# Strassen's method for the third layer, packed values as 64x32 matmuls, and a filler removed, in a one-core attention and MoE kernel

## The chip, the core and the metric

The kernel runs on one core of one Trainium2 chip. The core has TensorE (PE in the profile) for matmuls, VectorE (DVE), ScalarE (ACT) and GpSimd (POOL) for element work, and queues that issue DMA transfers between HBM and the on-chip SBUF; in this kernel the loads and stores are issued from SyncE (SP). Matmuls write to PSUM, which has eight banks of 128 partitions by 512 fp32 values here. The metric is the device time of one execution in microseconds (us), lower is better; it is given as the median of several runs.

## The reference

```python
def sm_attn(qq, kk, vv):                         # scale = 1/sqrt(64)
    s = scale * qq @ kk.transpose(0, 1, 3, 2)
    a = np.exp(s - max(s)); a = a / (sum(a) + 1e-9)
    return a @ vv
p_packed = sm_attn(p, k, v)                      # 8 x 8 heads, 32 packed rows, 576 tokens, depth 64
out = sm_attn(q, p_packed, p_packed)             # 8 x 8 heads, 576 tokens
x = out.transpose(0, 2, 1, 3).reshape(4608, 512)
h = x @ w_in                                     # layer 1: 512 -> 2048
x = (h * np.cos(h)) @ w_out                      # layer 2: 2048 -> 512
h = x @ w2_in                                    # layer 3: 512 -> 2048
return (h * tanh(softplus(h))) @ w2_out          # mish, then layer 4: 2048 -> 512
```

All data are fp32. The kernel makes a product of two fp32 matrices from three matmuls in a rounded fp32 form: each operand is split into a high part (a cast) and a low part (the subtraction of that cast), and high x high, high x low and low x high are added in PSUM. The helper `mm3` (lines 139 to 142) issues these three, so nearly all matmuls of the profile stand on lines 140, 141 and 142.

## The kernel before, in words

**Stage A** covers attention and layers 1 and 2. It runs 256 steps: 16 token blocks t of 288 tokens times 16 tiles s of 128 hidden features. A step issues `l1` (6 matmuls of 288 columns) and, three steps later (`LAG_A`), `l2` (12 matmuls of 288 columns). Between the two stands a chain for each step: an ACT pass (L709), two DVE passes (L711, L712), the sine on ACT (L718), a DVE product (L719), an ACT cast (L726) and a POOL subtraction (L729), whose result `gh` layer 2 needs. The attention output is never multiplied out before layer 1: the packed values of a batch entry (32 x 64 for each head) are multiplied with layer 1's weights first, in `w_unit` (L492, plain fp32), and ACT and DVE split the result (L503, L504) into the `wab` tiles that layer 1 reads. Loads, element passes and matmuls of attention, of these units and of the weight preparation are put into tables by step (`at_ld`, `at_ew`, `at_pe`); a scheduler that uses priorities then orders the instructions of each engine.

Weights of layers 3 and 4 are loaded, rounded and written to DRAM tiles (`ws`) in stage A (`pre2`), and late in stage A `w2_load` reads them back and splits them. Layer 3's 16 pieces then stay in eight `wab` tiles, layer 4's 16 in `wo` tiles. **Stage B** covers layers 3 and 4: 9 blocks of 512 tokens times 16 tiles of hidden features. A step has `l3` (12 matmuls of 512 columns), mish on ACT, a split, and three steps later `l4` (12 matmuls of 512 columns). So stage B has 9 x 16 x 24 = 3456 matmuls of 512 columns, half of them for layer 3. While it runs, the next token block's `x` is loaded from DRAM, split, and the results of a finished block are copied out of PSUM and stored.

Of the kernel before, what the change touches and what calls it, by code (L numbers as in the profile page):

```python
# [56 lines left out]
W_D = 0  # L57
X2_AT = 250
# [17 lines left out]
PERM = ((0, 1, 2, 3), (2, 3, 0, 1))  # L76


def build(tc, q, k, v, p, w1i, w1o, w2i, w2o, out):
    nc = tc.nc  # L80
    ctx = ExitStack()
    with ctx:
# [29 lines left out]
        mask = wpool.tile([128, 64], F32, name="mask")  # L112
        nc.vector.memset(mask, 0.0)
        for a in range(2):
            nc.vector.memset(mask[64 * a : 64 * a + 64, 32 * a : 32 * a + 32], 1.0)
# [40 lines left out]
        PS = {}  # L156
        PW = {}
        lastexp = [None]

        def k_unit(b, g, alloc_v):  # L160
# [135 lines left out]
            def s6_ew():  # L296
                if b not in PS:
                    PS[b] = ap.tile([128, 128], F32, tag="psp", bufs=3, name=nm("psp"))
                nc.scalar.copy(PS[b][64 * g : 64 * g + 64], st["xt"][64 * g : 64 * g + 64, :128])
                if (b // 2, g) not in PW:  # L300
                    PW[(b // 2, g)] = ap.tile([128, 2, 2, D], F32, tag=f"pw{g}", bufs=2 - g, name=nm("pw"))
                pw = PW[(b // 2, g)]
                for sp in range(2):
                    i = sp if par == 0 else 1 - sp
                    nc.vector.tensor_tensor(pw[:, i, sp], st["xt"][:, 64 * sp : 64 * sp + 64], mask, ALU.mult)
# [14 lines left out]
        def q_unit(t, pre=None):  # L320
# [28 lines left out]
            def s2_pe():  # L349
                st["s"] = [ring() for _ in range(2)]  # L350
                for l in range(4):
                    h = PERM[b % 2][l]
                    for g in range(2):
                        nc.tensor.matmul(  # L354
                            st["s"][g][32 * l : 32 * l + 32, :TT],
                            PS[b][64 * g : 64 * g + 64, 32 * l : 32 * l + 32],
                            st["kt"][64 * g : 64 * g + 64, TT * h : TT * h + TT],
                            start=True,
                            stop=True,
                        )  # L360
# [103 lines left out]
        whalf = {}  # L464

        def w_unit(pair, fg, hp, bp, fresh=False, m=None):
            st = {} if m is None else m
            g, i = hp // 2, hp % 2
            cs = []

            if fresh:
# [8 lines left out]
                cs = cs[:-1]  # L480
            else:

                def load():
                    st["m"] = ld_tile([128, 512])
                    nc.sync.dma_start(st["m"], w1s[(fg, hp)])

            def pe():
                if i == 0:
                    whalf[(bp, fg, g)] = ring()
                ps = whalf[(bp, fg, g)]  # L490
                pos = bp ^ i
                nc.tensor.matmul(  # L492
                    ps[64 * pos : 64 * pos + 64], PW[(pair, g)][:, i, pos], st["m"], start=True, stop=True
                )

            def ew():
                if i == 0:
                    return
                ps = whalf.pop((bp, fg, g))
                w = W1.get((2 * pair + bp, fg))  # L500
                if w is None:
                    w = W1[(2 * pair + bp, fg)] = wab_tile(bp, [128, 2, 2, 512], F32R)
                nc.scalar.copy(w[:, g, 0], ps)  # L503
                nc.vector.tensor_tensor(w[:, g, 1], ps, w[:, g, 0], ALU.subtract)  # L504

            return load, cs, pe, ew
# [16 lines left out]
        W2 = {}  # L523

        def w2_load(key):
            st = {}

            def load():
                st["r"] = ld_tile([128, 512])
                nc.sync.dma_start(st["r"], w2s[key])  # L530

            def hi():
                if key[0] == "i":
                    _, j, c = key
                    if j not in W2:
                        W2[j] = wab_tile(j // 4, [128, 2, 2, 2, 256], F32R)
                    v = W2[j][:, c].rearrange("p l a f -> p l (a f)")
                else:
                    v = WO[(2, key[1])] = wo_tile([128, 2, 512], F32R)
                st["v"] = v  # L540
                nc.scalar.copy(v[:, 0], st["r"])

            def lo():
                eng = nc.gpsimd if key[-1] % 3 == 0 else nc.vector
# [61 lines left out]
        place(stages, [PRO + Q0_T + i for i in range(2)] + [PRO + Q0 + i for i in range(6)], HP_PRO)  # L606
        for j in range(16):
            load, cs, pe, ew = w_unit(0, j // 4, j % 4, 0, True)
# [4 lines left out]
            at_pe(n, pe)  # L613
            at_ew(n, ew)
# [12 lines left out]
        for j in range(16):  # L627
            load, cs, pe, ew = w_unit(0, j // 4, j % 4, 1)
            n = W01[0] + int(W01[1] * j)
            at_ld(n - W_LD, load)  # L630
            at_pe(n, pe)
            at_ew(n, ew)
# [18 lines left out]
        for pair in range(3):  # L651
# [9 lines left out]
            for j in range(16):  # L661
                m = {}
                n = n0 + W_POS[pair][0] + int(W_POS[pair][1] * (j // 2 * 2 + 1))
                at_ld(n - W_LD - 1 + j % 2, w_unit(pair + 1, j // 4, j % 4, 0, m=m)[0])
                for bp in range(2):
                    _, _, pe, ew = w_unit(pair + 1, j // 4, j % 4, bp, m=m)
                    at_pe(n + W_D * bp, pe)
                    at_ew(n + W_D * bp, ew)
# [5 lines left out]
        n0 = 192  # L674
        for j in range(8):
            for c in range(2):
                n = n0 + 33 + 2 * j + c if j < 4 else n0 + 48 + 4 * (j - 4) + 2 + c
                load, hi, lo = w2_load(("i", j, c))
                at_ld(n, load)
                at_ew(n + 1, hi)  # L680
                at_ew(n + 2, lo)
# [233 lines left out]
```

## Time and profile before

| | before |
|---|---|
| median of 3 runs | 1654.02 us (1653.84 to 1654.74) |
| the profiled execution's own time | 1651.3 us |
| its span, first to last instruction | 1649.5 us |
| PE busy | 1588.2 us, 96% of the span |
| DVE, ACT, POOL busy | 717.9, 762.2 and 365.0 us |
| mean granted TensorE clock | 0.992 of full speed |

The span leaves out 1.8 us of the execution's own time. The median lies 2.7 us above the time of the profiled execution. A busy share says only how long an engine had work in flight; which engine sets the end is read from the chain that ended last and from the gaps of that engine.

### The profile page before, as it was taken

What the parts mean: (1) busy time and instruction counts of PE and PEld (TensorE: products, weight loads), DVE (VectorE), ACT (ScalarE), POOL (GpSimd) and SP (SyncE); (2) the same over time, 40 slices, a digit from 0 to 9 for tenths busy, and PEclk for the clock granted to TensorE, in tenths of its full rate; (3) what the DMA queues carried; (4) which work ended last, traced back from release to release, by engine and by line L of the source; (5) the groups of instructions that cost most, each with busy time, mean ns of one, the idle gap of its engine ahead of it and who ended that gap; (6) DMA issues with size and microseconds to landing.
All of it is one profiled execution on the core that took longest, in us unless ns stands there. A gap on an engine that the chain in (4) does not pass through costs nothing.

```text
span 1649.5 us, 25389 instructions
## 1 busy us (share of the span) xinstructions
PE 1588.2 (96%) x9568; PEld 1324.5 (80%) x9568; DVE 717.9 (44%) x1529; ACT 762.2 (46%) x1510; POOL 365.0 (22%) x376
## 2 busy tenths in 40 slices
PE   3879999999999999999999999999999999999999
PEld 1667777799878997889898888888888888888887
DVE  5986665666657666687761111111111111111111
ACT  3676576666656666667772222322222222222221
POOL 0552223343323333244660010101010101000000
PEclk9899999999999999999999999999999999999999
DMA  9979565533544343353340010101010101010000
GB/s 285 305 192 237 152 189 135 136 79 86 162 113 99 89 124 127 98 187 117 111 131 0 16 36 1 52 0 51 1 52 1 51 0 52 1 52 1 8 18 26
DMA packets 101115, 147.42 MB, mean 89 GB/s; under 512 B 25728, under 2 KB 51328, under 8 KB 100992
## 3 DMA queue, kind: packets, MB, share of 16 engines
q1 hardware_dynamic: 100992, 145.79, 31.1%
q8 instruction: 75, 1.23, 0.3%
q14 instruction: 48, 0.39, 0.1%
HBM read 114.29 MB, written 31.46 MB: 88 GB/s over the span
## 4 chain that ended last, share of the span: by engine, by line
PE 84%; DMA 7%; DVE 4%; ACT 2%; issue 2%; SPq 1%; POOL 0%; DVEq 0%; ACTq 0%; POOLq 0%
PE acc L140 15%; PE acc L141 14%; PE acc L142 14%; PE ps L140 12%; PE ps L141 11%; PE ps L142 11%; PE ps L492 3%; DMA kr<-in_k_dram 1%; DMA kr<-in_q_dram 1%; DMA raw<-in_moe_w_out_dram 1%; PE ps L354 1%; DMA ld<-ws 1%; PE ps L214 1%; PE ps L275 1%; DVE r L719 1%
## 5 line engine op out<-in xcount | busy, mean ns | idle before, releaser
L856 DVE TENSOR_TENSOR gh<-gg,gh 128x512 fp32r<-128x512 f32 x144 | 105.7, 734 | 623.6 <-ACT gh L855 623.5
L849 ACT ACTIVATE gg<-ps 128x512 f32<-128x512 f32 x144 | 86.1, 598 | 550.4 <-PE ps L142 550.4
L729 POOL TENSOR_TENSOR gh<-r,gh 128x288 fp32r<-128x288 f32 x256 | 215.6, 848 | 396.4 <-ACT gh L726 288.6
L141 PE MATMUL acc<-gh,wo 128*128 128x288 f32 x1024 | 301.9, 300 | 0.3
L142 PE MATMUL acc<-gh,wo 128*128 128x288 f32 x1024 | 297.8, 298 | 0.0
L140 PE MATMUL acc<-gh,wo 128*128 128x288 f32 x1024 | 284.3, 305 | 1.7 <-ACT gh L726 1.7
L141 PE MATMUL acc<-wo,gh 128*128 128x512 f32 x576 | 227.2, 394 | 0.0
L140 PE MATMUL acc<-wo,gh 128*128 128x512 f32 x576 | 226.7, 394 | 0.0
L142 PE MATMUL acc<-wo,gh 128*128 128x512 f32 x576 | 225.0, 391 | 0.0
L140 PEld LDWEIGHTS acc<-gh,wo 128*128 128x128 f32 x1024 | 184.7, 190 | 38.7 <-issue 18.0
L141 PEld LDWEIGHTS acc<-gh,wo 128*128 128x128 f32 x1024 | 194.6, 190 | 8.8 <-issue 4.6
L142 PEld LDWEIGHTS acc<-gh,wo 128*128 128x128 f32 x1024 | 193.4, 190 | 6.3 <-issue 4.6
L140 PE MATMUL ps<-aT,wab 128*128 128x288 f32 x512 | 160.5, 314 | 17.0 <-DVE r L719 10.9
L718 ACT ACTIVATE r<-r,halfpi 128x288 f32<-128x288 f32 x256 | 135.7, 535 | 78.4 <-DVE r L712 75.9
L709 ACT ACTIVATE ki<-ps,quarter 128x288 int32<-128x288 f32 x256 | 125.5, 496 | 83.4 <-PE ps L142 73.4
L141 PE MATMUL ps<-aT,wab 128*128 128x288 f32 x512 | 152.9, 299 | 0.0
L142 PE MATMUL ps<-aT,wab 128*128 128x288 f32 x512 | 152.5, 298 | 0.0
L719 DVE TENSOR_TENSOR r<-r,ps 128x288 f32<-128x288 f32 x256 | 113.9, 449 | 69.1 <-ACT r L718 68.7
L711 DVE SCALAR_TENSOR_TENSOR r<-ki,ps 128x288 f32<-128x288 int32 x256 | 113.9, 448 | 55.8 <-ACT ki L709 46.5
L140 PEld LDWEIGHTS ps<-aT,wab 128*128 128x128 f32 x512 | 97.9, 192 | 39.1 <-DVE r L719 20.2
L140 PEld LDWEIGHTS acc<-wo,gh 128*128 128x128 f32 x576 | 108.2, 188 | 25.1
L142 PEld LDWEIGHTS acc<-wo,gh 128*128 128x128 f32 x576 | 108.2, 188 | 24.8
(124 smaller groups left out, 2579.2 us busy)
## 6 DMA issues: line engine op xcount, KB each, us to landing
ld<-ws SPq DMA_DIRECT2D x96, 256.0 KB, 2.9
kr<-in_k_dram SPq DMA_DIRECT2D x64, 272.0 KB, 5.7
raw<-in_moe_w_out_dram SPq DMA_DIRECT2D x32, 512.0 KB, 4.8
kr<-in_q_dram SPq DMA_DIRECT2D x60, 272.0 KB, 5.5
x2d<-xo SPq DMA_DIRECT2D x64, 144.0 KB, 1.8
out_dram<-ld SPq DMA_DIRECT2D x36, 256.0 KB, 2.0
raw<-in_moe_w_in_dram SPq DMA_DIRECT2D x16, 512.0 KB, 5.7
ws<-tmp SPq DMA_DIRECT2D x32, 256.0 KB, 4.8
```

The lines of the kernel that those rows point to most:

```text
L140: nc.tensor.matmul(ps, l0, r0, start=first, stop=False)
L141: nc.tensor.matmul(ps, l0, r1, start=False, stop=False)
L142: nc.tensor.matmul(ps, l1, r0, start=False, stop=last)
L214: nc.tensor.matmul(st["s1"][x][32 * l : 32 * l + 32, :TT].rearrange("p (s a) -> p a s", a=9), st["pp"][64 * x : 64 * x + 64, 32 * h : 32 * ...
L492: nc.tensor.matmul(ps[64 * pos : 64 * pos + 64], PW[(pair, g)][:, i, pos], st["m"], start=True, stop=True)
L709: nc.scalar.activation(ki, st["h"], AF.Identity, bias=quarter, scale=1.0 / TWO_PI)
L711: nc.vector.scalar_tensor_tensor(r, ki, -TWO_PI, st["h"], ALU.mult, ALU.add)
L718: nc.scalar.activation(g, g, AF.Sin, bias=halfpi, scale=1.0)
L719: nc.vector.tensor_tensor(g, g, st["h"], ALU.mult)
L729: nc.gpsimd.tensor_tensor(gh[:, 1], st["g"], gh[:, 0], ALU.subtract)
L849: nc.scalar.activation(g, st["h"], AF.Mish)
L856: nc.vector.tensor_tensor(gh[:, 1], st["g"], gh[:, 0], ALU.subtract)
```

## The change

It has three parts.

**Layer 3 by Strassen's method** (in Winograd's form). The product of a 512 x 256 piece of the weights with 1024 tokens is cut into 2 x 2 blocks on each side. Instead of eight block products, seven are made from sums of blocks, and the four result blocks are sums of the seven. There are now four token blocks of 1024 and one of 512. For each, and for each of 8 pairs p of hidden tiles, `product` issues 7 x 6 matmuls (of 512 columns, in the last block of 256) where 48 stood for the same 1024 tokens. DVE adds the products out of PSUM. The hidden values of a block's second 512 tokens are kept in 16 `G` tiles, and layer 4 for them runs behind all pairs (`xs`, `g_split`, the loop over `f`). The weight sums are made in stage A by `w2_comb`, eight units, seven steps apart from step 180: two loads, four DVE sums, four splits into `raw` tiles and four writes to DRAM tiles `wst`. Stage B streams them: `ws_load` fetches 256 KB for each product into one of five `tmp` buffers, 280 times, and the load for product m+5 is issued behind product m. The sums of x are made by `x_units`, at the end of stage A for the first block, later in the second part of the block ahead.

**Packed values as 64x32 matmuls.** `PK` is one ACT copy of 128 x 128 per batch entry and group, without the mask and its DVE products. A unit now issues four matmuls with 64 rows and 32 columns of the array for one batch entry, or eight for two, where matmuls with 128 rows and 64 columns, half of them masked to zero, stood.

**A filler removed.** `gap_b`, 48 unused values per partition, is gone.

```diff
-X2_AT = 250
+X2_AT = 248
+COMB = (180, 7)
-PERM = ((0, 1, 2, 3), (2, 3, 0, 1))
+PERM = ((0, 2, 1, 3), (1, 3, 0, 2))
...
-                    pw = PW[(b // 2, g)]
-                    nc.vector.tensor_tensor(pw[:, i, sp], st["xt"][:, 64 * sp : 64 * sp + 64], mask, ALU.mult)
+                PK[(b, g)] = ap.tile([128, 128], F32, tag=f"pk{g}", bufs=4, name=nm("pk"))
+                nc.scalar.copy(PK[(b, g)], st["xt"][:, :128])
...
-                nc.tensor.matmul(
-                    ps[64 * pos : 64 * pos + 64], PW[(pair, g)][:, i, pos], st["m"], start=True, stop=True
-                )
+                for x in range(4):
+                    for b in bs:
+                        for l, h in enumerate(PERM[b % 2]):
+                            if l == x:
+                                r = 64 * (h % 2)
+                                nc.tensor.matmul(
+                                    st[b][32 * l : 32 * l + 32],
+                                    PK[(b, g)][r : r + 64, 32 * l : 32 * l + 32],
+                                    ms[h // 2]["m"][r : r + 64],
...
+        def w2_comb(j):
...
+            def sums():
+                c0, c1 = st["c"]
+                a11, a21, a12, a22 = c0[:, :, :128], c0[:, :, 128:], c1[:, :, :128], c1[:, :, 128:]
+                sa, sb = [tmp_tile([128, 2, 2, 128]) for _ in range(2)]
+                nc.vector.tensor_tensor(sa[:, 0], a21, a22, ALU.add)
+                nc.vector.tensor_tensor(sa[:, 1], sa[:, 0], a11, ALU.subtract)
+                nc.vector.tensor_tensor(sb[:, 1], a11, a21, ALU.subtract)
+                nc.vector.tensor_tensor(sb[:, 0], a12, sa[:, 1], ALU.subtract)
...
+            def split(k):
+                    r = tp.tile([128, 2, 2, 2, 128], F32R, tag="raw", bufs=2, name=nm("hl"))
...
+                                nc.scalar.copy(d, src)
...
+                                (nc.gpsimd if k < 2 else nc.vector).tensor_tensor(d, src, h, ALU.subtract)
...
+                    nc.sync.dma_start(t, r[:, :n].bitcast(F32))
...
-                    W2[j] = wab_tile(j // 4, [128, 2, 2, 2, 256], F32R)
...
+        def x_sums(i, a):
...
+                nc.vector.tensor_tensor(t1, b12, b11, ALU.subtract)
+                nc.vector.tensor_tensor(t2, b22, t1, ALU.subtract)
+                nc.vector.tensor_tensor(t3, b22, b12, ALU.subtract)
+                nc.vector.tensor_tensor(t4, b21, t2, ALU.subtract)
+                raws[(i, a)] = (b11, b21, t2, t3, t4, t1, b22)
...
+                nc.scalar.copy(x[:, a, 0, :n], src)
+                (nc.gpsimd if k % 2 else nc.vector).tensor_tensor(x[:, a, 1, :n], src, x[:, a, 0, :n], ALU.subtract)
...
-        bp.tile([128, 48], F32, name="gap_b")
...
+        def ws_load(m):
+            if m < NQ:
+                WS[m] = tp.tile([128, 2, 2, 128], F32R, tag="tmp", bufs=TMP_BUFS, name=nm("ws"))
+                nc.sync.dma_start(WS[m].bitcast(F32), WST[divmod(m % 56, 7)])
...
+        def product(i, p, k, ps, n):
+            m = 56 * i + 7 * p + k
+            w, x = WS.pop(m), X[(i, k)]
+            for a in range(2):
+                mm3(ps, w[:, 0, a], w[:, 1, a], x[:, a, 0, :n], x[:, a, 1, :n], a == 0, a == 1)
+            ws_load(m + TMP_BUFS)
...
+                ps = prod(2)
+                u2 = add(ct("u2", 1), ps, m1)
+                sub()
...
```

A unit of packed values for two batch entries, on PE, a little behind the middle of stage A. In the kernel before its rows are those of L492: two calls write two PSUM tiles, then two more.

```order
L142 MATMUL acc3_1050_5406<-gh_1075_5562,wo_164_746 128x288
L492 MATMUL ps_1096_5666<-ld_1077_5568,pw_785_3899 64x512
L492 MATMUL ps_1097_5668<-ld_1077_5568,pw_785_3899 64x512
L492 MATMUL ps_1096_5666<-ld_1086_5612,pw_785_3899 64x512
L492 MATMUL ps_1097_5668<-ld_1086_5612,pw_785_3899 64x512
L140 MATMUL acc0_1047_5403<-gh_1083_5602,wo_178_799 128x288
```

The same unit in the changed kernel, where its calls have line 483:

```order
L483 MATMUL ps_1096_5706<-ld_1077_5604,pk_784_3939 32x512
L483 MATMUL ps_1096_5706<-ld_1086_5652,pk_784_3939 32x512
L483 MATMUL ps_1096_5706<-ld_1077_5604,pk_784_3939 32x512
L483 MATMUL ps_1096_5706<-ld_1086_5652,pk_784_3939 32x512
L138 MATMUL acc2_1049_5441<-gh_1083_5642,wo_175_798 128x288
L136 MATMUL acc3_1050_5442<-gh_1083_5642,wo_175_798 128x288
L483 MATMUL ps_1097_5707<-ld_1077_5604,pk_985_5127 32x512
L483 MATMUL ps_1097_5707<-ld_1086_5652,pk_985_5127 32x512
L136 MATMUL ps_1103_5746<-aT_1005_5213,wab_706_3538 128x288
...
L483 MATMUL ps_1097_5707<-ld_1077_5604,pk_985_5127 32x512
L483 MATMUL ps_1097_5707<-ld_1086_5652,pk_985_5127 32x512
L137 MATMUL acc3_1050_5442<-gh_1083_5642,wo_175_798 128x288
```

Four calls in one place have become eight narrower ones in three places. The four calls of one batch entry write one PSUM tile, two from the upper row half of the array and two from the lower, to different partitions. Over the program the units of two batch entries stand in 38 places on PE; 36 visits of them are in the trace of before.

The next rows are of ACT, at the end of the fourth block from the last of stage A (the `xo` rows copy that block out). Before:

```order
L726 CAST gh_1737_9153<-r_1728_9109 128x288
L718 ACTIVATE r_1757_9235<-r_1757_9235,halfpi_88 128x288
L726 CAST gh_1752_9205<-r_1736_9150 128x288
L750 COPY xo_1741_9163<-acc0_1627_8576 128x288
L718 ACTIVATE r_1763_9275<-r_1763_9275,halfpi_88 128x288
L750 COPY xo_1743_9169<-acc2_1629_8578 128x288
L726 CAST gh_1758_9238<-r_1751_9202 128x288
L709 ACTIVATE ki_1767_9305<-ps_1766_9284,quarter_90 128x288
```

In the changed kernel, at the same block's end; lines 740, 749 and 757 are the chain's 709, 718 and 726, and `hl` is a `raw` tile of `w2_comb` (line 548):

```order
L757 CAST gh_1804_9435<-r_1786_9374 128x288
L781 COPY xo_1793_9393<-acc0_1653_8732 128x288
L781 COPY xo_1795_9399<-acc2_1655_8734 128x288
L757 CAST gh_1812_9475<-r_1803_9432 128x288
L548 CAST hl_1813_9479<-tmp_1791_9387 128x2x256
L548 CAST hl_1822_9526<-tmp_1792_9388 128x2x256
L749 ACTIVATE r_1819_9517<-r_1819_9517,halfpi_84 128x288
L740 ACTIVATE ki_1825_9552<-ps_1824_9531,quarter_86 128x288
L757 CAST gh_1820_9520<-r_1811_9472 128x288
L548 CAST hl_1828_9560<-ld_1775_9308 128x256
L740 ACTIVATE ki_1831_9586<-ps_1830_9565,quarter_86 128x288
```

Casts into `raw` tiles stand between the chain's passes. There are two such buffers, so `hl_1828` takes the place of `hl_1813`, five rows earlier.

The last rows are of DVE, near the end of stage A. Before (L545 is the split of weights in `w2_load`, `r_2050` belongs to the last step):

```order
L711 SCALAR_TENSOR_TENSOR r_2041_10761<-ki_2040_10759,ps_2039_10738 128x288
L719 TENSOR_TENSOR r_2034_10721<-r_2034_10721,ps_2032_10698 128x288
L712 TENSOR_SCALAR r_2041_10761<-r_2041_10761 128x288
L545 TENSOR_TENSOR wo_2021_10648<-ld_2014_10611,wo_2021_10648 128x512
L711 SCALAR_TENSOR_TENSOR r_2050_10801<-ki_2049_10799,ps_2048_10778 128x288
L719 TENSOR_TENSOR r_2041_10761<-r_2041_10761,ps_2039_10738 128x288
L712 TENSOR_SCALAR r_2050_10801<-r_2050_10801 128x288
L545 TENSOR_TENSOR wo_2028_10688<-ld_2023_10652,wo_2028_10688 128x512
```

In the changed kernel (742, 743 and 750 are the chain's 711, 712 and 719; 574 is the old 545; 810 to 813 are the sums of x; `r_2133` belongs to the last step):

```order
L742 SCALAR_TENSOR_TENSOR r_2127_11079<-ki_2126_11077,ps_2125_11056 128x288
L810 TENSOR_TENSOR ld_2136_11122<-xr_2123_11046 128x512
L750 TENSOR_TENSOR r_2117_11029<-r_2117_11029,ps_2115_11006 128x288
L743 TENSOR_SCALAR r_2127_11079<-r_2127_11079 128x288
L574 TENSOR_TENSOR wo_2103_10956<-ld_2098_10924,wo_2103_10956 128x512
L742 SCALAR_TENSOR_TENSOR r_2133_11113<-ki_2132_11111,ps_2131_11090 128x288
L574 TENSOR_TENSOR wo_2111_10996<-ld_2106_10964,wo_2111_10996 128x512
L743 TENSOR_SCALAR r_2133_11113<-r_2133_11113 128x288
L811 TENSOR_TENSOR ld_2137_11123<-xr_2124_11051,ld_2136_11122 128x512
L812 TENSOR_TENSOR ld_2138_11124<-xr_2124_11051,xr_2123_11046 128x512
L750 TENSOR_TENSOR r_2127_11079<-r_2127_11079,ps_2125_11056 128x288
L813 TENSOR_TENSOR ld_2139_11125<-xr_2124_11051,ld_2137_11123 128x512
```

Sums of x stand between the last passes of the chain, and the first ones read `xr` tiles that are loaded there.

## Rows read from the trace of the kernel before

**Rows 1.** The page, its parts 1 and 4.

```profile
PE 1588.2 (96%) x9568; PEld 1324.5 (80%) x9568; DVE 717.9 (44%) x1529; ACT 762.2 (46%) x1510; POOL 365.0 (22%) x376
...
PE 84%; DMA 7%; DVE 4%; ACT 2%; issue 2%; SPq 1%; POOL 0%; DVEq 0%; ACTq 0%; POOLq 0%
```

**Rows 2.** PE's timeline (start us, us, ...): the start and the end of stage B.

```profile
851.12 0.39 PE L140 MATMUL ps<-xr,wab 128*128 128x512 f32 x1
...
1645.56 0.39 PE L142 MATMUL acc<-wo,gh 128*128 128x512 f32 x1
```

**Rows 3.** Busy time by stretch; the last columns are clock, DMA share, GB/s.

```profile
60.00:100.00 40.00, 32.85 (x219) 23.27 (x219) 36.39 (x71) 27.40 (x55) 19.94 (x18) 0.99 0.81 250
600.00:815.00 215.00, 207.29 (x1519) 185.71 (x1518) 160.34 (x343) 147.95 (x311) 92.92 (x97) 0.99 0.41 133
815.00:851.00 36.00, 36.00 (x274) 36.00 (x273) 29.86 (x52) 27.69 (x62) 25.18 (x24) 1.00 0.45 142
851.00:1650.00 799.00, 794.94 (x3459) 648.99 (x3457) 118.92 (x166) 206.39 (x341) 42.72 (x33) 1.00 0.08 23
```

**Rows 4.** Timeline of PE: 14 neighbouring matmuls of 288 columns.

```profile
844.77 0.29 PE L140 MATMUL acc<-gh,wo 128*128 128x288 f32 x1
...
846.49 0.29 PE L141 MATMUL acc<-gh,wo 128*128 128x288 f32 x1
```

**Rows 5.** Timeline of PE: two visits of packed-value matmuls, with the next row.

```profile
499.52 1.94 PE L492 MATMUL ps<-ld,pw 128*64 128x512 f32 x8
501.39 0.40 PE L140 MATMUL ps<-aT,wab 128*128 128x288 f32 x1
...
507.20 1.08 PE L492 MATMUL ps<-ld,pw 128*64 128x512 f32 x4
508.21 0.66 PE L140 MATMUL acc<-gh,wo 128*128 128x288 f32 x3
```

**Rows 6.** All packed-value matmuls of this form: durations in ns, first and last start.

```profile
L492 PE MATMUL ps<-ld,pw x224: 592/592/644, 155.2 to 693.0; 128*64 128x512 f32 x112
```

**Rows 7.** Timeline of PE: smaller matmuls of attention, with a next row.

```profile
489.20 0.63 PE L275 MATMUL ps<-ld,tmp 128*32 128x64 f32 x26
...
503.97 0.71 PE L214 MATMUL ps<-kt,pp 64*32 64x288 f32 x16
504.61 0.67 PE L140 MATMUL acc<-gh,wo 128*128 128x288 f32 x3
```

**Rows 8.** Groups by line: busy us and mean ns, idle before.

```profile
L856 DVE TENSOR_TENSOR gh<-gg,gh 128x512 fp32r<-128x512 f32 x144 | 105.7, 734 | 623.6 <-ACT gh L855 623.5
L504 DVE TENSOR_TENSOR wab<-ps,wab 128x512 fp32r<-128x512 f32 x64 | 43.6, 687 | 26.3 <-ACT wab L503 25.7
L545 DVE TENSOR_TENSOR wab<-ld,wab 128x512 fp32r<-128x512 f32 x8 | 9.0, 1124 | 1.8 <-ACT wab L541 1.8
L541 ACT CAST wab<-ld 128x512 fp32r<-128x512 f32 x16 | 9.3, 618 | 0.9 <-DMA ld<-ws 0.8
L545 POOL TENSOR_TENSOR wab<-ld,wab 128x512 fp32r<-128x512 f32 x8 | 10.8, 1353 | 9.7 <-ACT wab L541 5.9 <-DVE r L711 2.9 <-DVE r L712 0.9
```

**Rows 9.** DMA issues: KB each, median us to landing.

```profile
ld<-ws SPq DMA_DIRECT2D x96, 256.0 KB, 2.9
...
ws<-tmp SPq DMA_DIRECT2D x32, 256.0 KB, 4.8
...
ws<-wo SPq DMA_DIRECT2D x4, 256.0 KB, 7.7
```

**Rows 10.** Timeline of PE: a gap in stage A and what follows.

```profile
800.42 0.29 PE L141 MATMUL acc<-gh,wo 128*128 128x288 f32 x1
802.87 0.61 PE L140 MATMUL ps<-aT,wab 128*128 128x288 f32 x1 [2.16 <-DVE r L719]
...
805.20 0.44 PE L140 MATMUL ps<-aT,wab 128*128 128x288 f32 x1
805.44 0.44 PE L141 MATMUL ps<-aT,wab 128*128 128x288 f32 x1
```

More of the change, by code (lines that the diff above doesn't have):

```diff
@@ L463, in build, with w_load @@
         w1s = {}
[L464 to L469, printed above, removed]
+        def w_load(fg, hp, fresh=False):
+            st = {}
             if fresh:
@@ L790, in build, with x_load, f @@
-        for kc in range(4):
-            load, split = x2_unit(0, kc)
-            at_ld(X2_AT + kc, load)
-            at_ew(X2_AT + kc + 2, split)
+        X = {}
+        raws = {}
+        def x_load(i, a):
+            def f():
+                n = 1024 if i < 4 else 512
+                rs = []
+                for kc in (a, 2 + a):
+                    r = tp.tile([128, n], F32, tag="raw", bufs=2, name=nm("xr"))
+                    lo, hi = 1024 * i, 1024 * i + n
+                    for t in range(lo // TT, (hi - 1) // TT + 1):
+                        u, z = max(lo, t * TT), min(hi, t * TT + TT)
+                        nc.sync.dma_start(r[:, u - lo : z - lo], x2d[t][:, kc, u - t * TT : z - t * TT])
+                    rs.append(r)
+                raws[(i, a)] = rs
+            return f
@@ L795, in build @@
+        for u, f in enumerate(x_units(0)):
+            a, u = divmod(u, 9)
+            if u == 0:
+                at_ld(X2_AT + 5 * a, f)
+            else:
+                at_ew(X2_AT + 5 * a + 1 + (u + 1) // 2, f)
         NA = NT * NF
@@ new lines, in build, with ring_b, acc_b @@
+        ringn = [0]
+        def ring_b(i):
+            if i % 2 == 0:
+                return ring()
+            ringn[0] += 1
+            return psum.tile([128, 512], F32, tag=f"acc{ringn[0] % 4}", bufs=1, name=nm("rb"))
+        def acc_b(x):
+            return accs() if x % 2 == 0 else [ring() for _ in range(4)]
+        def product(i, p, k, ps, n):
[4 more added lines that the diff above has]
+            ws_load(m + TMP_BUFS)
@@ new lines, in split, with gh_tile, l4_subs, sub @@
+        def split(gh, c, cols, eng=None):
+            nc.scalar.copy(gh[:, 0, cols], c)
+            (eng or nc.vector).tensor_tensor(gh[:, 1, cols], c, gh[:, 0, cols], ALU.subtract)
+        def gh_tile():
+            return bp.tile([128, 2, BT], F32R, tag="gh2", bufs=4, name=nm("gh2"))
+        def l4_subs(ac, f, gh):
+            def sub(j):
+                def run():
+                    w = WO[(2, f)]
+                    o = 128 * j
+                    mm3(ac[j], gh[:, 0, o : o + 128], gh[:, 1, o : o + 128], w[:, 0], w[:, 1], f == 0, f == NF - 1)
+                return run
+            return [sub(j) for j in range(4)]
@@ L870, in evac2 @@
+        def evac2(ac, r0):
             for j in range(4):
```

324 lines of the change are left out of this document (174 added, 150 removed).

## The prediction

> **What bounds the kernel now.** I read the page first, then busy time by stretch, then PE's timeline. The chain that ended last is PE for 84%, and PE is busy for 1588.2 of 1649.5 us [rows 1]; so the question is how many matmuls there are, what one costs, and where PE stands still. By stretch the two stages differ [rows 3]. From 851 to 1650 us PE is busy for 794.94 of 799 us while DVE has 118.9 and ACT 206.4, and DMA moves 23 GB/s: stage B is a bare stream of matmuls. Its first starts at 851.12, its last at 1645.56 us [rows 2], so 3455 intervals take 794.4 us, 0.2299 us each, with no pause that shows. A matmul taken out there is 0.23 us gained. From 600 to 815 us it is another matter: PE has 207.3 of 215 us, but DVE 160.3 and ACT 148.0, and in the last 36 us of stage A DVE has 29.9 and ACT 27.7 [rows 3]. Each step's chain ACT, DVE, ACT, DVE, ACT, POOL stands between layers 1 and 2, and the gap at 800 us shows what happens when it is late: PE waited for DVE from 800.42 to 802.87, and its matmuls then stood 0.24 us apart, still at 805.44 [rows 10], where 0.132 is usual [rows 4]: TensorE was at the lower of its two clock levels. Work put there on DVE and ACT is not free.
>
> **Layer 3, the gain.** Before: 1728 matmuls of 512 columns. After: in each of four blocks 8 pairs x 7 products x 6 = 336, so 1344 of 512 columns, and 336 of 256 columns in the last block; layer 4 keeps its 1728. No row shows 256 columns. Fourteen neighbouring matmuls of 288 columns are 13 x 0.132 us apart [rows 4]; a straight line through 288 (0.132) and 512 (0.230) gives 0.118 at 256. Bounds: half of a 512 is 0.115, and a 288 is 0.132, so 336 of them cost 38.6 to 44.4, taken 39.7. Stage B after: (1344 + 1728) x 0.2299 + 39.7 = 706.3 + 39.7 = 746.0 us against 794.7 before (3456 x 0.2299): **-48.6** (-49.7 to -43.9).
>
> The Trainium skill ("TensorE: Matmul & The Clock Gate", the paragraph on back-to-back matmuls) gives N/2.4 GHz plus 2.5 ns, so 216 ns at 512; the trace has 230 for the rounded fp32 here, 14 more. By the page's figure 256 columns cost 0.109 and the sum would be 3 us lower.
>
> **What has to hide in stage B.** A pair has 42 matmuls of layer 3 and 24 of layer 4, 66 x 0.23 = 15.2 us. DVE does in it seven additions from PSUM at 0.69 (nearest row L504) and two splits at 0.73 (L856) [rows 8]: 6.3 us. ACT has seven passes of about 0.62 (L541), 4.3 us. Both hide. Each product needs its own 256 KB, one every 15.2/7 = 2.17 us; 121 GB/s, where the stretch from 60 to 100 us moved 250 [rows 3]. A load goes out behind product m for product m+5, four products or 8.7 us ahead, and a 256 KB load lands in 2.9 us [rows 9]. At the first pair of a block no layer 4 stands between, a product is 6 x 0.23 = 1.38 us and the lead 5.5; in the last block a pair is 42 x 0.118 + 24 x 0.23 = 10.5 us, a product 1.5, the lead 6.0. All are above 2.9. In the second part of a block layer 4 is 192 matmuls, 44 us, under which the next block's loads, sums and splits go. I take +2 us for starts and ends of the four second parts (0 to 10).
>
> **Packed values.** The 224 records of this form start from 155.2 to 693.0 us [rows 6]: 192 belong to the three pairs of batch entries, in 36 visits, 14 of 8 records and 22 shorter; a call leaves two records. A visit of 8 records takes 1.87 us to the next matmul's start, one of 4 takes 1.01 [rows 5]: two calls on the two column halves run together, four need two rounds. Before: 14 x 1.87 + 22 x 1.01 = 48.4 us. After, the calls are 64x32, eight fit the array at once, and the order has 38 visits. The trace has such matmuls: the 16 records of L214 (eight calls, 288 columns) take 0.64 us to the next start [rows 7], one round. So 38 x 1.01 = 38.4, **-10.0**. An ideal order with 24 visits would give -24; the splitting costs the rest. The units of entry 1 stand in 9 visits before and after, those of entry 0 under the waits at the start: 0 for both (-4 to +3). The masked DVE products that go, the copy on ACT and the filler: nothing, since DVE and ACT idle for a quarter of the stretch where they stand; without that cover it is less than 3 us either way.
>
> One thing differs from L214: there the two row halves of the array write different PSUM tiles, here the four calls of one entry write one tile from both halves. L275 shows four column groups at once into one tile (26 records of 64 columns in 0.56 us to the next start, rows from 489.20) [rows 7], but with all 128 rows. No row has two row halves into one bank. The Trainium skill ("TensorEngine Tiling (Array Packing)", Restrictions and Gotchas, PSUM pressure) says that different row tiles cannot access the same PSUM bank at the same time. By it these calls would take two rounds; what that costs is the third case below, from the rows.
>
> **Weight sums in stage A.** Eight units from step 180 to 236, roughly the stretch 600 to 815 us. Each has four half-size sums and two subtractions on DVE (five of half length at some 0.4, half of 0.73, and one of 0.73: 2.7 us), casts on ACT (2.3) and two subtractions on POOL (2.7, at 1.35 from L545) [rows 8]: 22, 18 and 22 us in all. The `w2_load` splits of layer 3 that go had 9.0 on DVE (8 x 1.124), 9.9 on ACT (16 x 0.618) and 10.8 on POOL. Net +13, +9 and +11 us: DVE would stand at 173 of 215 us, with cover in the average but not everywhere. The writes are 8 x 1.79 MB = 14.7 MB, 68 GB/s on top of 133 over that stretch, below the 250 seen [rows 3]. The new wait is ACT's: a cast into a `raw` tile waits until the tile two before has been subtracted and written. That is about 1.35 + 4.8 = 6.1 us [rows 8, 9]. Between `hl_1813` and `hl_1828` ACT has one cast (0.62) and three passes of 288 columns, which I put at 0.5 each (0.35 to 0.62 from L541 by length or in full): 2.1 us. So it would be held for 4.0 us, and behind it stand the next passes of the chain. Layer 2 runs three steps late, 3 x 18 x 0.132 = 7.1 us [rows 4], in which the chain's own passes must fit too; I let it absorb all but 0.6. One such place in each unit, 8 x 0.6: **+5** (0 if all is absorbed, 32 if nothing is).
>
> **End of stage A.** DVE gets eight sums and eight subtractions of x, 16 x 1.12 = 17.9 us [rows 8], and loses about four weight splits, 4.5. Its idle time in the last 36 us is 6.1 [rows 3], so some 7 of the 13 have no cover, and the last chain passes stand behind them in DVE's order. PE has first products to do in the meantime, whose x is ready early for half of the sum. I take **+4** (0 to 13).
>
> **The sum.** -48.6 - 10.0 + 2 + 5 + 4 = -47.6 us. The profiled execution took 1651.3 us, 1.8 more than its span: 1603.7 after. The median shown is 1654.02, 2.7 above that execution: **1606 us** in the same terms.
>
> **How else it could go.** *The preparation stalls* (0.20): of the 4.0 us of each held cast 2.5 are felt and not 0.6, 15 us more, and three gaps over 2 us bring the lower clock, which cost at least 1.2 us from 802.87 to 805.44 [rows 10]: +19 to +20, 1626. For it speaks DVE at 75% of the stretch and 83% of the last 36 us, against it that PE can take other work. *Two rounds for one bank* (0.12): the 32 visits of pairs with four calls or more cost 0.86 us more each (1.87 - 1.01), the 7 such of entry 1 and 4 of entry 0 too: 43 x 0.86 = 37, so 1643, and the narrow calls are then slower than the wide ones by 27. *The stream of weights is the bound* (0.05), which ends on the other side: with five buffers five products take at least a landing and one product's own time. In full blocks PE waits from a landing of 5 x 2.17 - 1.38 = 9.5 us on, in the last block from 5 x 1.5 - 0.7 = 6.8. At 9.8 us the loss is 224 x 0.066 + 56 x 0.6 = 48 us and the whole gain is gone; at 10.3 us it is 224 x 0.166 + 56 x 0.7 = 76, so 1682. The row says 2.9, and the slowest 256 KB of the trace 7.7 [rows 9]; at 7.7 only the last block waits, 56 x 0.18 = 10 us. For it speaks that one queue issues everything, loads of x and stores too. *No gain from the narrow calls* (within the first case's range): 10 us more, 1616.
>
> **How the numbers follow.** First case 0.63, its own range 1592 to 1620 from the bounds above; the others 0.20, 0.12 and 0.05. The likeliest time is 1606. The range takes in the second case and most of the way to the third: 1590 to 1636. A change under 0.2% (3.3 us) is about what a measurement cannot tell from none. Faster needs all but the fourth case: 0.93; the same 0.01; slower 0.06, from the fourth case and from several costs at their upper bounds together.
>
> **What would show it.** Right: stage B is a stream again, 0.23 us apart, and at its last block 0.118; no wait of PE for a `ws` load; eight L483 calls in one round, about 1.0 us; after the first product about 750 us to the end. Wrong: gaps of PE on `ws` tiles (fourth case); 1.9 us for visits of four calls (third); waits of PE for the chain between 600 and 851 us, with ACT held by writes into `wst` (second). If a 256-column matmul takes as long as 288, stage B is 4.7 us longer.

## The result, and the profile after

The changed kernel takes 1624.74 us (median of 4 runs, 1623.2 to 1627.3), the kernel before on the same footing 1654.38: ratio 0.9821, 95% interval 0.9804 to 0.9838, so 29.6 us less. The forecast was 1606 with a range of 1590 to 1636. The sign and the range hold; the sum of the likeliest case is 19 us too low, and the time is that of its second case (1626).

The page of the changed kernel, parts 1 and 6 (answering [rows 1] and [rows 9]); its span is 28.1 us shorter:

```profile
span 1621.4 us, 27105 instructions
...
PE 1533.1 (95%) x9776; PEld 1292.4 (80%) x9776; DVE 961.3 (59%) x1894; ACT 813.2 (50%) x1640; POOL 393.5 (24%) x402
...
ws<-wst SPq DMA_DIRECT2D x280, 256.0 KB, 2.6
ld<-ws SPq DMA_DIRECT2D x96, 256.0 KB, 3.3
...
wst<-hl SPq DMA_DIRECT2D x24, 512.0 KB, 3.1
```

Busy time by stretch, columns as in [rows 3]:

```profile
600.00:815.00 215.00, 195.07 (x1468) 172.98 (x1462) 169.64 (x357) 144.34 (x310) 96.90 (x104) 0.98 0.57 194
815.00:863.00 48.00, 44.75 (x323) 43.27 (x323) 37.60 (x70) 33.38 (x74) 24.06 (x24) 1.00 0.44 140
863.00:1620.00 757.00, 747.88 (x3464) 624.92 (x3464) 344.00 (x529) 256.90 (x457) 69.43 (x50) 1.00 0.38 122
```

In the first stretch PE has 195 of 215 us where it had 207, DVE 170 where it had 160. Most of the gain lies behind 863 us and the losses ahead of it. To see where, I cut both traces by progress and not by time: stage A has 4608 matmuls of 288 columns, 18 for each step, so the start of every such matmul says which step PE has reached. Us between the starts, and for the last column to the start of the last 512-column matmul:

```
                        steps 0-24  24-192  192-240  240 to last    span
before                       101.9   533.1    135.0        832.7  1649.5
changed                      108.8   527.2    151.6        786.9  1621.4
difference                    +6.9    -5.9    +16.6        -45.8   -28.1
```

(+0.2 comes ahead of the first of these matmuls.) A trace is one execution, and a column varies by itself. Up to step 192 the kernel before and run 5 below issue the same instructions in the same order on PE, DVE and ACT, but run 5 has 105.2 and 534.3 in the first two columns; run 4, in the order of the changed kernel, has 110.7 and 527.0. So a difference of 3 us in one column says little. The forecast had nothing in the first column, -10 in the second, +5 in the third with what lies ahead of step 192, and -42.6 in the last (-48.6 + 4 + 2).

**Stage B.** Timeline of PE in a block of 1024 tokens and in the last block (answering [rows 2] and [rows 4]):

```profile
1100.18 0.39 PE L136 MATMUL rb<-wab,ws 128*128 128x512 f32 x1
...
1103.81 0.39 PE L137 MATMUL ps<-wo,gh 128*128 128x512 f32 x1
```

```profile
1560.93 0.28 PE L136 MATMUL ps<-wab,ws 128*128 128x256 f32 x1
...
1561.53 0.28 PE L138 MATMUL ps<-wab,ws 128*128 128x256 f32 x1
```

Seventeen neighbours of 512 columns lie 16 x 0.227 us apart, six of 256 columns 5 x 0.12 (mean over the block 0.118, as forecast). But 0.2267, the mean from 1000 to 1400 us, is not the 0.2299 of before, and that was forecast by no step.

**Packed values.** Four calls of one batch entry, into one PSUM tile from both row halves, and eight calls of two entries (answering [rows 5]):

```profile
267.62 1.06 PE L483 MATMUL ps<-ld,pk 64*32 64x512 f32 x8
268.62 0.80 PE L136 MATMUL acc<-gh,wo 128*128 128x288 f32 x4
...
275.01 1.09 PE L483 MATMUL ps<-ld,pk 64*32 64x512 f32 x16
276.03 0.40 PE L137 MATMUL acc<-gh,wo 128*128 128x288 f32 x1
```

Both take 1.0 us to the next start, one round. That settles the third case (two rounds, 1.87 us): it is out.

**The third column.** ACT's waits from 620 us to the end of stage A, at 882 and at 851 us (columns: waiter, released by, us in total, times, longest), changed kernel and then the kernel before:

```profile
ACT r L749 <- DVE r L743: 31.1, 35, 3.1
ACT tmp L427 <- DMA raw<-in_moe_w_out_dram: 11.9, 9, 2.5
ACT hl L548 <- DMA wst<-hl: 6.9, 5, 3.3
...
ACT hl L548 <- DVE tmp L533: 5.1, 4, 1.7
```

```profile
ACT r L718 <- DVE r L712: 23.9, 43, 1.8
...
ACT tmp L439 <- DMA raw<-in_moe_w_out_dram: 4.3, 7, 1.2
```

The largest wait is for the chain's own pass on DVE, and it grew from 23.9 to 31.1 us. The 6.9 us are the wait that the forecast named: a cast into a `raw` tile stands until the tile two before is written. The 11.9 us it did not name: the conversions of layer 4's weights (L427, steps 199 to 242) load into the same two buffers. DVE's part of the conversions (L428) stands for these loads too, 9.1 us in this stretch where it was 2.3. The longest gap, on PE, on DVE and on POOL:

```profile
708.36 0.29 PE L138 MATMUL acc<-gh,wo 128*128 128x288 f32 x1
712.85 0.51 PE L136 MATMUL ps<-aT,wab 128*128 128x288 f32 x1 [4.20 <-DVE r L750]
713.16 0.44 PE L137 MATMUL ps<-aT,wab 128*128 128x288 f32 x1
713.40 0.44 PE L138 MATMUL ps<-aT,wab 128*128 128x288 f32 x1
...
716.28 0.36 PE L137 MATMUL acc<-gh,wo 128*128 128x288 f32 x1
```

```profile
706.43 0.44 DVE L742 SCALAR_TENSOR_TENSOR r<-ki,ps 128x288 f32<-128x288 int32 x1
706.79 1.46 DVE L534 TENSOR_TENSOR tmp<-ld 128x256 f32<-128x256 f32 x1
708.17 0.41 DVE L428 TENSOR_SCALAR cvt<-raw 128x512 int32<-128x512 int32 x1
708.51 0.41 DVE L533 TENSOR_TENSOR tmp<-tmp,ld 128x256 f32<-128x256 f32 x1
708.85 0.30 DVE L743 TENSOR_SCALAR r<-r 128x288 f32<-128x288 f32 x1
709.06 0.44 DVE L742 SCALAR_TENSOR_TENSOR r<-ki,ps 128x288 f32<-128x288 int32 x1
...
710.03 1.49 DVE L535 TENSOR_TENSOR tmp<-ld,tmp 128x256 f32<-128x256 f32 x1
...
712.36 0.44 DVE L750 TENSOR_TENSOR r<-r,ps 128x288 f32<-128x288 f32 x1
```

```profile
706.54 1.42 POOL L385 TENSOR_TENSOR aT<-tmp,aT 128x576 fp32r<-128x576 f32 x1 [0.32 <-ACT aT L384]
709.70 1.54 POOL L550 TENSOR_TENSOR hl<-tmp,hl 128x512 fp32r<-128x512 f32 x1 [1.73 <-ACT hl L548]
```

PE waits for the chain. Between the chain's two passes L742 and L743 on DVE, 2.4 us apart, stand two sums (L534, L533) and a conversion (L428). The sine follows on ACT from 709.53 to 710.06 us, but L750, for which PE waits, starts only at 712.36, behind a third sum (L535) and other passes. All three sums are of half length, which the forecast put at 0.4 us: L533 takes 0.41, but L534 and L535 take 1.46 and 1.49. These two run beside a POOL pass, and so it is over the whole trace: of the 32 sums of weights, the 14 that run beside no POOL pass take 0.38 to 0.42 us, the 18 others 0.41 to 1.50 and 0.83 on average. With DVE's splits of these sums, its share of the eight units is 31 us where the forecast had 22. That long passes and POOL's work coincide is all that the trace shows; no run moved POOL's work. Behind the gap PE's matmuls stand 0.24 us apart until about 716 us, as at 802.87 in [rows 10]; the granted clock from 713.0 to 716.4 is 0.50, the lower of its two levels.

**The seam.** DVE and PE where layers 2 and 3 meet:

```profile
868.00 1.39 DVE L743 TENSOR_SCALAR r<-r 128x288 f32<-128x288 f32 x1
869.32 1.78 DVE L811 TENSOR_TENSOR ld<-xr,ld 128x512 f32<-128x512 f32 x1
871.03 0.68 DVE L812 TENSOR_TENSOR ld<-xr,xr 128x512 f32<-128x512 f32 x1
871.63 0.44 DVE L750 TENSOR_TENSOR r<-r,ps 128x288 f32<-128x288 f32 x1
```

```profile
872.12 0.50 PE L136 MATMUL ps<-wab,ws 128*128 128x512 f32 x1 [1.40 <-DVE r L750]
...
876.60 0.62 PE L137 MATMUL ps<-wab,ws 128*128 128x512 f32 x1 [2.27 <-DVE wab L825]
...
887.21 0.50 PE L136 MATMUL ps<-wab,ws 128*128 128x512 f32 x1 [1.86 <-DVE c L946]
```

The chain's pass L743 ends at 869.4 and the sine behind it on ACT at 870.0, but the chain's last pass on DVE, L750, starts at 871.63, behind two sums of x; DVE has no pause from 858 to 878 us.

### The profile page after: what moved, and what is told of

Read it like the earlier page. It is cut to its first block, busy times and chain, and to the rows that moved or that the text cites. A ratio compares the mean times of both kernels' runs of the same rounds, so it can differ in the third digit from the quotient of the medians.

```text
span 1621.4 us, 27105 instructions
## 1 busy us (share of the span) xinstructions
PE 1533.1 (95%) x9776; PEld 1292.4 (80%) x9776; DVE 961.3 (59%) x1894; ACT 813.2 (50%) x1640; POOL 393.5 (24%) x402
## 5 line engine op out<-in xcount | busy, mean ns | idle before, releaser
L957 ACT ACTIVATE c<-c 128x512 f32<-128x512 f32 (+1 forms) x96 | 53.8, 561 | 242.6 <-DVE c L946 242.3
L750 DVE TENSOR_TENSOR r<-r,ps 128x288 f32<-128x288 f32 x256 | 114.6, 449 | 63.2 <-ACT r L749 62.2
L742 DVE SCALAR_TENSOR_TENSOR r<-ki,ps 128x288 f32<-128x288 int32 x256 | 114.0, 447 | 60.0 <-ACT ki L740 46.8
L757 ACT CAST gh<-r 128x288 fp32r<-128x288 f32 x256 | 108.4, 429 | 50.1 <-DVE r L750 28.4
L743 DVE TENSOR_SCALAR r<-r 128x288 f32<-128x288 f32 x256 | 122.7, 482 | 3.8
L137 PE MATMUL acc<-wo,gh 128*128 128x512 f32 x320 | 125.0, 391 | 0.0
L136 PE MATMUL acc<-wo,gh 128*128 128x512 f32 x320 | 124.9, 390 | 0.0
L136 PE MATMUL ps<-wab,ws 128*128 128x512 f32 (+1 forms) x336 | 119.5, 356 | 5.1 <-DVE r L750 2.5
L138 PE MATMUL acc<-wo,gh 128*128 128x512 f32 x320 | 124.2, 389 | 0.0
```

Source lines behind the costliest of these rows:

```text
L136: nc.tensor.matmul(ps, l0, r0, start=first, stop=False)
L137: nc.tensor.matmul(ps, l0, r1, start=False, stop=False)
L138: nc.tensor.matmul(ps, l1, r0, start=False, stop=last)
L742: nc.vector.scalar_tensor_tensor(r, ki, -TWO_PI, st["h"], ALU.mult, ALU.add)
L743: (nc.gpsimd if n % C_MOD in C_POOL else nc.vector).tensor_scalar(r, r, 1.570796, -4.712388, ALU.min, ALU.max)
L750: nc.vector.tensor_tensor(g, g, st["h"], ALU.mult)
```

## The experiments

Each time is a median, with its ratio to the kernel before as it ran beside it (1655.0 to 1655.4 us). After each stands the row of the table of progress where it says more.

**1. No weight sums in stage A**

```diff
-            load, fs = w2_comb(j)
-            at_ld(COMB[0] + COMB[1] * j, load)
...
+                t = w2s[("i", j, k % 2)].rearrange("p (h a f) -> p h a f", h=2, a=2)
+                nc.sync.dma_start(WS[m].bitcast(F32), t)
```

> The changed kernel without the weight sums in stage A: no loads, sums, splits or writes of w2_comb; stage B streams the rounded weights themselves, 280 loads of 256 KB as before, so the output is not the reference's. Theory (the making of the sums stalls stage A, through the two raw buffers it shares with the conversion of layer 4's weights, and brings the lower clock after the gaps): 15 to 20 us less than the changed kernel, 1605 to 1610 us, PE's waits between 620 and 850 us mostly gone, stage B as it was. Rival (the lost time lies at the seam between the stages and in stage B): at most 6 us less, 1619 or more.

Measured: 1602.85 us, ratio 0.9681 (0.9655 to 0.9707): 22 less than the changed kernel, a little more than the theory had. Steps 192 to 240 take 131.0 us and not 151.6; the last column stays at 785.5. So making the sums costs some 20 us, all of it there, and the seam is a loss of its own.

**2. No stream of weights**

```diff
-            w, x = WS.pop(m), X[(i, k)]
+            w, x = WS[m % TMP_BUFS], X[(i, k)]
...
-            ws_load(m + TMP_BUFS)
```

> The changed kernel with only the first five of the 280 weight loads of stage B; each product reads one of these five tiles again, so the output is not the reference's. Theory (the stream is hidden: loads land in 2.6 us, with a lead of 5 us and more): the same time within 3 us, and 512-column matmuls 0.227 us apart as before. Rival (the stream costs something, in the two gaps of 1.1 and 2.3 us at the first products or in the spacing): 4 to 10 us less.

Measured: 1621.42 us, 0.9799 (0.9772 to 0.9826), against 0.9821 (0.9804 to 0.9838): the intervals overlap widely. The last column is 784.7, 2.2 less than with the stream. 512 columns stay 0.2267 us apart. The stream is hidden to within some 3 us, and is not what changed the spacing.

**3. Strassen and the filler's removal, packed values as before**

```diff
-                for x in range(4):
-                    for b in bs:
-                        for l, h in enumerate(PERM[b % 2]):
...
+                nc.tensor.matmul(
+                    ps[64 * pos : 64 * pos + 64], PW[(pair, g)][:, i, pos], st["m"], start=True, stop=True
+                )
...
```

> The changed kernel with the packed values as before (128x64 matmuls, masked, the mask and its DVE products, a unit for each half). Theory (the narrow calls save 8.6 us on the pairs and 1.2 on entry 1, but the units of entry 0, which now wait for two converted weight tiles, lose 6 at the start): 2 to 6 us more than the changed kernel, 1627 to 1631. Rival (the whole gain of 10 us that was forecast is there and the loss at the start has another cause, such as the x of the clock): 9 to 12 us more, 1634 to 1637.

Measured: 1623.44 us, 0.9818 (0.9794 to 0.9842): no difference from the changed kernel, where the theory had 2 to 6 us more. By progress: 101.9 us for steps 0 to 24 (108.8 with the narrow calls) and 535.1 for 24 to 192 (527.2). The narrow calls lose at the start about what they win on the pairs. Steps 192 to 240 take 148.3 us, though ACT's two waits through the raw buffers are 7.9 and 3.5 us here and not 11.9 and 6.9.

**4. The fillers put back**

```diff
+        wpool.tile([128, 64], F32, name="gap_m")
...
+        bp.tile([128, 48], F32, name="gap_b")
```

> The changed kernel with the filler of 48 values before stage B's tiles put back, and an unused tile of 64 values where the mask stood. Theory (addresses cost nothing; the 0.2267 us between 512-column matmuls, 0.2299 before, comes from the different operands): the same time within 3 us and 0.2267 still. Rival (the addresses of the tiles set the spacing): 0.2299 again, 3072 x 0.0032 = 10 us more, 1635.

Measured: 1628.90 us, 0.9836 (0.9808 to 0.9864), between the two expectations; the intervals overlap. The trace tells more: layer 3's matmuls stay 0.2265 us apart, layer 4's go from 0.2267 to 0.2292, 0.2317 and 0.2262 for the three of `mm3` (mean 0.2290), and the last column grows by 5.0 us to 791.9; 1728 x 0.0023 = 4.0. Only layer 4 loads weights from a tile (`gh2`) that the filler moves. Run 3 has the mask's tile and not the filler, and 0.2267 throughout: it is the filler.

**5. The kernel before without its filler**

```diff
-        bp.tile([128, 48], F32, name="gap_b")
```

> The kernel before without its filler of 48 values ahead of stage B's tiles, nothing else changed. Theory (the place of stage B's own tiles sets the spacing of the matmuls that read them): layer 4's matmuls, which load weights from these tiles, go from 0.231 to 0.227 us (1728 x 0.0038 = 6.6 us) and the 768 of layer 3 whose x lies there from 0.233 to 0.227 (5.1 us): 11 to 12 us less than before, 1642 to 1643. Rival (the filler alone does nothing, the changed operands do): the same as before within 3 us.

Measured: 1642.17 us, 0.9923 (0.9900 to 0.9945): 13 less, as the theory said. Layer 3's first and last matmul of one step whose x lies in `xh`, before and without the filler:

```profile
980.60 0.39 PE L140 MATMUL ps<-xh,wab 128*128 128x512 f32 x1
...
983.16 0.40 PE L142 MATMUL ps<-xh,wab 128*128 128x512 f32 x1
```

```profile
981.89 0.39 PE L140 MATMUL ps<-xh,wab 128*128 128x512 f32 x1
...
984.38 0.39 PE L142 MATMUL ps<-xh,wab 128*128 128x512 f32 x1
```

11 intervals: 2.56 us, 0.2327 each, against 2.49, 0.2264. The last column falls from 832.7 to 821.4. So in the kernel before 11 us hang on a line that I costed at nothing. With run 3 this splits the change: the filler alone gives 13 us (ratio 0.9923), Strassen's method and the filler together give 30 (0.9818), so Strassen's method some 17 net, and the narrow calls on top nothing that shows.

**6. Entry 0's narrow units in halves**

```diff
...
-                at_pe(n, pe)
+                at_pe(W0_STEP[j - 1], lambda pe=pe: pe(0))
+                at_pe(n, lambda pe=pe: pe(1))
```

> The changed kernel with the units of batch entry 0 issued in halves, each as soon as its one converted weight tile is there, as before; all other units stay whole. Theory (at the start the whole units wait for two converted tiles and hold PE's order): 4 to 6 us less than the changed kernel, and the 250th matmul of 288 columns at about 111 and not 117 us. Rival (the start is slower because of the order that the scheduler finds, not because of that wait): within 2 us, and the 250th stays at 116 to 120 us.

Measured: 1626.85 us, 0.9821 (0.9796 to 0.9847), no gain; steps 0 to 24 take 109.6 us. The theory of the wait for two converted tiles is not borne out: what steps 8 to 16 gain (37.1 us against 41.8), steps 0 to 8 lose (42.3 against 38.2). It is not ruled out either: the 250th matmul starts at 113.0 us, between the two expectations, and steps 0 to 8 vary by themselves (38.4 us in the kernel before, 41.3 in run 5, in one order).

**7. Layer 4's conversions early**

```diff
-PRE_AT = (43, ..., 171, 171, 172, 199, 203, 204, 205, 205, 206, 207, 208, 219, 221, 222, 223, 236, 237, 242, 241, 238)
+PRE_AT = (43, ..., 171, 171, 172, 173, 56, 60, 64, 68, 72, 76, 80, 84, 112, 116, 120, 132, 138, 144, 150, 156)
```

> The changed kernel with the 16 conversions of layer 4's weights moved from steps 199 to 242 to steps 56 to 156 and the last one of layer 3 from 199 to 173, so that the two raw buffers serve the weight sums alone from step 180 on. Theory (the stalls come from the shared raw buffers: conversions wait for loads that wait for the sums to be written): 10 to 15 us less than the changed kernel, and ACT's waits for raw loads behind 620 us gone. Rival (DVE and ACT are simply too full there, or the work is as dear where it goes): at most 5 us less.

Measured: 1620.37 us, 0.9780 (0.9751 to 0.9810): 4 less, as the rival said, and the interval touches that of the changed kernel; but by progress both are right. Steps 192 to 240 take 136.7 us and not 151.6, and among ACT's waits from 620 to 882 us are these:

```profile
ACT r L749 <- DVE r L743: 34.0, 41, 2.4
ACT hl L548 <- DVE tmp L533: 8.9, 6, 2.8
...
ACT hl L548 <- DMA ld<-ws: 6.8, 3, 3.6
...
ACT tmp L427 <- DMA raw<-in_moe_w_in_dram: 2.1, 1, 2.1
...
ACT hl L548 <- DMA wst<-hl: 0.8, 1, 0.8
```

The two DMA waits through the raw buffers, 18.8 us in the changed kernel, are 2.9. But steps 24 to 192 now take 540.6 and not 527.2: the conversions are as dear where I put them. This trace is of the slowest of the four executions, 7.4 us above their median; run 8, with the conversions at the same steps and a trace 1.3 us above its median, has 138.9 and 543.8.

**8. Also the first sums of x from step 240**

```diff
...
-X2_AT = 248
+X2_AT = 240
...
```

> The run above with the sums of x for the first token block begun at step 240 instead of 248. Theory (DVE, without a pause from 858 to 878 us, sets the end of stage A): another 5 to 8 us less than the run above, and no gap of PE over 1 us between the last matmuls of layer 2. Rival (the sums only move to steps where they delay the chain as much): within 3 us of the run above.

Measured: 1618.55 us, 0.9770 (0.9739 to 0.9801). The total does not tell it from run 7, as the rival said; the last column does, 777.5 against 788.2, and PE's waits behind 862 us are these two, none over 1 us:

```profile
874.31 0.40 PE L137 MATMUL acc<-gh,wo 128*128 128x288 f32 x1 [0.53 <-POOL gh L760]
...
876.76 0.40 PE L137 MATMUL acc<-gh,wo 128*128 128x288 f32 x1 [0.57 <-POOL gh L760]
```

**9 and 10. The conversions at steps 98 to 165, or packed into 144 to 163** (edits as in 7 and 8, with other numbers in `PRE_AT`)

> The changed kernel with the conversions of layer 4's weights spread over steps 98 to 165, the last of layer 3 at 173, and the first block's sums of x from step 240. Theory (the shared raw buffers cost 17 us behind step 192; the conversions are dear at steps 56 to 84, 11 us in the two runs before, and nearly free at 112 to 160): 14 to 20 us less than the changed kernel, 1605 to 1611. Rival (they cost as much wherever they go): no better than the run that had them at 56 to 156, 1616 to 1620.

> As the run beside it, but with all 16 conversions of layer 4's weights packed into steps 144 to 163, where PE runs at 19.2 to 24 us per 8 steps and DVE and ACT have room. Theory: 12 to 20 us less than the changed kernel. Rival (packed so close they wait for the two raw buffers and hold DVE and ACT, as the sums did behind step 192): within 5 us of the changed kernel, with steps 144 to 168 up to 10 us slower.

Measured: 1613.32 us, 0.9741 (0.9721 to 0.9762), and 1613.98, 0.9756 (0.9737 to 0.9774). Both beat the changed kernel, by 11 us, less than I expected of either. Steps 24 to 192 take 533.9 and 537.6 us (the second in a trace 3.9 us above its run's median): the conversions cost 7 to 10 us in the middle of stage A and 13 to 17 at the steps of runs 7 and 8.

**11. The narrow calls alone, on the kernel before**

```diff
-PERM = ((0, 1, 2, 3), (2, 3, 0, 1))
+PERM = ((0, 2, 1, 3), (1, 3, 0, 2))
...
-                    PS[b] = ap.tile([128, 128], F32, tag="psp", bufs=3, name=nm("psp"))
+                PK[(b, g)] = ap.tile([128, 128], F32, tag=f"pk{g}", bufs=4, name=nm("pk"))
...
```

> The kernel before with the packed values as 64x32 matmuls alone; layer 3 and the filler as before. Theory (8.6 us saved on the pairs and 1.2 on entry 1, 4 to 8 lost in the first 24 steps): 2 to 6 us less than before, 1648 to 1652, and stage B's spacing 0.230 as before. Rival (the forecast 10 us): 1643 to 1645. Second rival (the place of the tiles, moved by the mask's 64 values, sets the spacing): 0.227 and 11 us more.

Measured: 1653.19 us, 0.9982 (0.9971 to 0.9993): 2 to 3 us less, as the theory said. Steps 24 to 192 take 523.9 us, 9.2 less than before; steps 0 to 24 take 109.1, 7.2 more. Stage B is unchanged (832.7, spacing 0.230), so the mask's place plays no part there.

**12. As run 9, but entry 0 with the wide masked calls**

```diff
...
-PERM = ((0, 2, 1, 3), (1, 3, 0, 2))
+PERM = ((0, 1, 2, 3), (1, 0, 3, 2))
...
+                if b == 0:
+                    PW[g] = ap.tile([128, 2, D], F32, tag=f"pw{g}", bufs=1, name=nm("pw"))
...
+            def half(i):
+                if i == 0:
+                    st[0] = ring()
+                nc.tensor.matmul(st[0][64 * i : 64 * i + 64], PW[g][:, i], ms[i]["m"], start=True, stop=True)
...
```

> The run with the conversions at steps 98 to 165, and besides it batch entry 0 alone as before: masked 128x64 matmuls, each issued as soon as its one converted tile is there (the heads of odd entries are reordered so that pairs still fill the array at once). Theory (the narrow whole units of entry 0 cost 4 to 7 us in the first 24 steps, which the kernel with all units as before did not lose): 4 to 7 us less than that run, 1606 to 1609, with steps 8 to 24 at 64 to 66 us instead of 72. Rival (the start's loss comes with the order of everything there, as when the units were halved): within 3 us of 1613.

Measured: 1607.35 us, 0.9718 (0.9696 to 0.9741): 6 less than run 9 (4 by the ratios, whose intervals overlap), 17 less than the changed kernel and 48 less than the kernel before, the best here apart from run 1, which leaves the sums out. Steps 0 to 24 take 104.6 us (run 9: 110.4).

## Why the prediction was right, and where its sum was off

**Layer 3, right.** The counts hold, 256 columns cost 0.118, and no product waits for the stream (run 2). At the spacing without the filler the part is worth 3456 x 0.2267 - (3072 x 0.2267 + 39.7) = 783.5 - 736.1 = 47.4 us, forecast 48.6.

**The filler, wrong.** "The filler: nothing" is 11 us of the last column in the kernel before (run 5) and 5 in the changed one (run 4), where layer 4 alone has an operand behind it.

**Packed values, right on the pairs, wrong at the start.** Pairs took 48.3 us and take 39.8, -8.5 for a forecast of -10.0; with entry 1 it is -9.2 by progress (run 11, one trace). The units of entry 0, "0 (-4 to +3)", cost some 7: nine traces with narrow calls whole at the start have 108.8 to 111.9 us for steps 0 to 24, four with wide calls there 101.9 to 105.2. The Trainium skill ("TensorEngine Tiling (Array Packing)", Restrictions and Gotchas, PSUM pressure) says that different row tiles cannot access the same PSUM bank at the same time. Two rounds would have made 1.87 us of a visit of four calls; the trace has 1.00, so no time is lost by that rule here. Why narrow calls are dearer at the start is open: run 6, without the wait for two tiles, gained nothing, and wide calls take most of it back (run 12, which also reorders heads).

**Weight sums, the step that failed most.** Forecast +5 (0 to 32); run 1 gives about 20. The named wait is there (6.9 us), but the step looked at the sums alone, and it put their DVE passes at 22 us where they take 31. With the conversions away the stretch takes 136.7 us (run 7), with the sums away 131.0 (run 1), with both 151.6, and before, with the conversions alone, 135.0: either fits, both together do not. The waits through the two raw buffers went from 4.3 to 18.8 us of ACT and back to 2.9. Run 7 takes the conversions' passes on DVE and ACT out of the stretch as well as their loads, so how much is the buffers and how much the fuller DVE is not separated. For the DVE speaks the longest gap, where its passes stand between the chain's, and run 3, whose stretch takes 148.3 us with 11.4 us of the two waits; a third buffer was not tried. (In the forecast's working 8 x 1.79 MB is 14.3 and not 14.7; the 68 GB/s hold, since a unit writes 1.835 MB.)

**End of stage A, right in kind, too small.** Forecast +4 (0 to 13). The last column gained 45.8 us, where 58.6 is due by its matmuls (794.7 - 736.1): 12.8 are lost, at the upper bound, nearly all at the seam: DVE had no pause for 20 us there, and run 8, which begins the sums of x earlier, takes 9 of them back.

**The sum.** Forecast -47.6, -28.1 in the spans. Against the forecast stage B is 12.0 better (-58.6 for -48.6 + 2), the packed pairs are 0.8 worse, the start 7.1, the weight sums 14.9 (16.6 + 3.3 ahead of step 192, for 5) and the seam 8.8: -47.6 - 12.0 + 0.8 + 7.1 + 14.9 + 8.8 = -28.0. Of the 12.0, 9.8 are the closer spacing of 3072 matmuls (0.0032 us each), which no step forecast, and 2 the starts and ends that cost nothing that shows. That the time lands on the second case is luck: that case had 19 to 20 us for the preparation, where 15 beyond the sum were lost, and the start's and the seam's losses (16) stand against 12 of unforeseen gain. The range does not hang on the filler: with it back (run 4) the time is 1628.9.

## What to carry to other kernels

When work is moved into a stage that is nearly full, list who else uses each buffer and each engine that it takes, and read the waits of both users in the trace: here the sums and the conversions, which share two buffers and a busy DVE, fitted alone and cost 15 us together. Take the price of a pass from a stretch where the other engines are as busy as they will be: sums put at 0.4 us took 0.83 on average beside POOL's work. Cut traces by progress (the starts of a counted instruction) and not by time, since a total of -3 us hid -9 and +7, and cut a second trace of the same order to see how much a column varies by itself. Price an unused tile by a run without it before calling it nothing: the matmul spacing of the tiles behind it is one look at the timeline.

## What the runs showed of the hardware

A filler of 48 values (192 bytes) per partition ahead of the tiles that matmuls read changed the spacing of 512-column matmuls by up to 3%: 0.2333 with it and 0.2267 without where the moving operand lies behind it, 0.2304 and 0.2267 on average where the loaded weights do; matmuls with neither operand there stayed at 0.2267 in the same run. Which property of the address it is was not tried. And four 64x32 matmuls from both row halves into different partitions of one PSUM tile ran in one round, 1.00 us for four calls as for eight in two tiles (1.02). DVE passes with SBUF operands alone ran longer beside POOL's: in the changed kernel's trace the chain's L743 (128 x 288) took 0.26 to 0.31 us in the 123 places without a POOL pass beside it, and up to 1.40, 0.65 on average, in the 133 others; L742 and L750, which read PSUM, took at most 0.46 either way.
